# Attention with two window patterns and a gated unit: larger gated blocks, smaller convolution parts, and a new instruction order

## The chip, the cores and the metric

The kernel runs on one core of a Trainium2 chip. A core has TensorE (PE, matrix products), VectorE (DVE), ScalarE (ACT), GpSimd (POOL) and SyncE (SP, which here only issues DMAs), each with its own instruction queue, and 16 DMA engines. The metric is the device time of one execution in microseconds, the median of several runs; lower is better.

## The reference

Eight batches, eight heads, 576 positions, 64 numbers a head. Heads 0 to 3 attend to the last 32 positions, heads 4 to 7 to every fourth of the last 128. The result, 512 numbers a position, goes into a gated unit: a causal convolution over five positions, a channel at a time, through a sigmoid, times a product with `w_val`, and the whole through `w_out`.

```python
rel = pos[:, None] - pos[None, :]
mask_plain = (rel >= 0) & (rel < window)                       # window = 32
mask_dil = (rel >= 0) & (rel < window * dilation) & (rel % dilation == 0)   # dilation = 4
...
attn = np.exp(scores)
attn = attn / (np.sum(attn, axis=-1, keepdims=True) + 1e-09)
return np.matmul(attn, v).astype(np.float32)
...
x = np.ascontiguousarray(attn_out.transpose(0, 2, 1, 3)).reshape(B, S, H * D)
...
for k in range(K):                                             # K = 5
    gate_pre += conv_w[k][None, None, :] * xp[:, k:k + S, :]
gate = 1.0 / (1.0 + np.exp(-gate_pre))
val = x @ w_val
return (gate * val @ w_out).astype(np.float32)
```

## The kernel before

The kernel is written as a list of tasks. A task (`Task`) has a name, the engines that can do it with a planned duration on each, the tasks it depends on, and the buffers it uses (`Ten`, one of a small class of equal buffers whose sizes stand in `TUNE['n']`). `Plan` gives each task an engine, a place and its buffers. It can search an order itself (`run`); here it follows one that is written out, `ORDER`: 825 words, each a task's number and the letter of its engine (`p` PE, `a` ACT, `d` DVE, `g` POOL, `s` SP). The order in `ORDER` is the order of each engine's instructions; between engines, semaphores make a task wait for what it needs. `place` keeps a clock for each engine from the planned durations. These serve to choose a buffer (the one that comes free first), and to decide in `fill` where the constant products go: while the planned PE clock is below `TUNE['warm']` and a gap is planned, PE multiplies the zero tile `warm` (512 columns) into a PSUM buffer that is free.

PSUM is held as three double banks (`ps2`, called `pd` in the profile) and two single ones (`ps1`, `pu`).

For each batch two attention halves run, `plain` (heads 0 to 3) and `dilated` (heads 4 to 7). Both load q and k (`load_qk`, L832), turn them on PE (L977 plain, L1071 dilated), copy them to SBUF (`copy`, L908 ACT, L910 DVE, L912 POOL), make scores in parts of 64 rows by 128 columns of the array (L1001, L1113), take the exponential on ACT (`softmax_half`, L931), and multiply by the mask. A dilated mask is a product on DVE (L942); a plain one is either that or two selections on POOL (L814, L816 in `band`). Then follow the products with V (L1014; L1127 and L1136), the division on DVE (L1024, L1025; L1148, L1149), and a transpose back (L1034; L1158, L1161) into `xT`, which holds the attention's result with channels on partitions.

V reaches the plain half in two ways. For batches 0 and 1 (`FAST = 2`) it is loaded in rows of four positions (L846, L849) and spread to positions by products with a shifted identity (`plain_v`, L871 and L877), in two tasks of 16 products. For the others a slower load (L839) puts it there at once, and POOL clears the part ahead of the sequence (L964). V of the dilated half is loaded (L893, L899) and cast on POOL (L912).

`gated` works on half a batch, 288 positions, and two of the four groups of 128 channels at a time, so 32 times. The convolution (L1189) is 20 products with diagonal 64x64 parts, four in the array at once, of 288 columns; `conv_diag` holds the diagonals. ACT takes a tanh (L1199). The value products (L1207) are eight of 288 columns, and DVE joins both into `ya` (L1217). `outputs` takes 128 positions at a time: four products of 512 columns (L1234), an eviction on ACT (L1242) or DVE (L1244), a store (L1248).

`weights` loads `w_val`, `w_out` and the convolution's weights (L1259, L1299, L1301) and casts them; rows and columns of the weights are put in an order that fits the halves in which the convolution leaves the channels.

Of the kernel before, what the change touches and what calls it, by code (L numbers as in the profile page):

```python
# [9 lines left out]
BF16 = mybir.dt.bfloat16  # L10
# [227 lines left out]
 'warm': 45.0,  # L238
 'stall': 0.601,
 'ahead': 7.06,  # L240
# [49 lines left out]
 'n': {'vf': 4,  # L290
       'ps2': 3,
       'ps1': 2,
       'qk': 5,
       'vp': 2,
       'va': 4,
       'vb': 3,
       'vab': 2,
       'vbb': 2,
       'qTp': 2,
       'kTp': 1,  # L300
       'qTd': 3,
       'kTd': 3,
       'et': 13,
       'xn': 5,
       'gate': 7,
       'osb': 15,
# [6 lines left out]
30s 2g 11d 8d 29s 9d 67s 118s 16a 0g 4a 3g 6d 1d 7d 5g 66s 40p 42p 10d 15g 41a 43a 14g 119s 12g  # L313
36p 38p 39d 37a 17a 55p 48p 68s 44p 49a 56a 59p 45a 69s 74p 31s 60a 46d 75d 76a 77p 32s 127p 79a
125p 126d 78a 95p 91p 33s 128d 131p 96a 57d 84p 156s 129p 85a 80p 130d 92a 155s 70p 50d 132a 93g
157s 86d 81a 13d 61d 137p 133p 34g 82d 72p 134a 97d 71a 35g 47p 158s 73d 51p 138a 121s 18p 52d
144p 122s 62p 145a 120s 58p 148p 63d 163p 149a 208s 53p 19a 164d 87p 165a 20g 83p 98p 64p 88d 166p
65a 23s 21s 94p 54a 161p 150d 207s 99d 168a 124g 167a 180p 135d 162d 184p 181a 173p 89p 123g 245s
174a 159p 139d 185a 146d 186d 244s 151p 160a 90d 147p 100p 152d 136p 140p 24g 101a 169p 218p 141d
170a 220p 106p 219a 171d 22g 102p 107a 175d 114p 103a 221d 153p 293s 292s 176p 115a 182d 172p 216p  # L320
108p 177d 217a 154a 214p 27s 109d 187p 183p 215a 116p 188d 226p 142p 25s 227a 117d 178p 246s 233p
222p 143d 234a 248p 223a 179d 251p 250d 249a 189p 104p 252d 253a 265p 105d 110p 266a 190d 258p
111a 254p 267d 299p 329s 303p 259a 199p 304d 255a 28g 260g 195p 235d 200a 191p 228d 196a 193p 256g
26d 300d 112p 192a 194d 330s 305p 113d 197p 306a 301p 198d 717p 247g 209s 211s 269p 718a 237p 210s
257p 261p 238a 732p 262d 270a 331s 203p 733a 271g 224d 336p 204a 302d 333p 239d 337a 322p 335d
723p 323a 338d 212g 415s 334a 272p 268p 729p 724a 273d 213g 225p 263p 730a 229p 343p 230d 339p
726p 340a 264d 344a 240p 414s 727d 307p 354p 308a 231p 236p 274p 355a 241d 205p 332g 378s 275a
294s 341g 201p 206d 232a 345d 276p 295s 356g 202d 296s 346p 277a 342p 242p 347d 738p 377s 243a
350p 311p 309d 318p 351a 720p 739d 319a 416s 352d 421p 312a 324d 418p 423a 422d 388p 420a 353p
297g 357p 278p 358d 419a 499s 298g 721a 288p 279d 428p 289a 359p 389d 280p 429a 360d 435p 281a  # L330
424p 430g 384p 390p 436a 385d 290p 313d 391a 437g 348p 425a 463s 291d 310p 314p 386p 315d 282p
387a 349d 379s 417g 439p 407p 320d 381s 440a 735p 500s 283d 408a 321p 316p 441d 736a 325p 462s
392p 317a 326d 396p 747p 393a 409d 380s 442p 397a 327p 748d 464s 438p 361p 328a 394d 362a 741p
465s 443d 403p 284p 404a 426d 365p 466s 742d 285a 369p 398d 366a 431p 370a 427p 473p 432d 503p
551s 506p 548s 504a 383g 505d 373p 507a 722s 382g 501s 471p 374a 286p 472d 508a 405d 469p 287d
474a 395p 399p 520p 400d 513p 750p 514a 470d 521a 410p 751d 524p 547s 509p 525a 401p 406p 433p
402a 411d 371p 526g 510a 475p 372d 375p 476a 467g 434a 481p 636s 376d 477p 482a 632s 412p 558p
413d 367p 478a 559a 483d 502g 585s 560p 368d 488p 584s 561a 468g 492p 753p 522d 493a 515g 479d
444p 586s 754a 523p 527p 445d 363p 489a 511g 528d 556p 480p 484p 557a 364d 446p 490d 450p 447a
485d 744p 451a 494d 491p 756p 745a 554p 495p 555a 454p 496d 458p 455a 757d 562p 497p 563a 516p  # L340
758s 486p 498d 634s 512p 459a 588p 725s 517d 591p 589a 759p 593a 487d 550s 587g 456p 592d 752s
746s 518p 457d 633s 460p 519a 670s 637g 760d 549s 743s 590a 762p 755s 461d 553g 573p 763d 598p
594p 595a 780p 599a 596g 669s 529p 452p 781a 574a 448p 600g 453d 749s 530a 564d 768p 449d 765p
769a 770s 609p 766d 566p 605p 764s 567a 771p 740s 782s 606a 641p 767s 772d 535p 610a 607g 635s
539p 536a 611d 531p 642d 540a 552g 575d 543p 532a 568d 577p 643p 578a 671s 537p 544a 579d 761s
608p 644a 612p 538d 533p 613d 645p 601p 597p 646a 777p 602d 778a 565p 639p 569p 534d 640a 673p
570d 676p 674a 783p 675a 677d 678a 576p 571p 784d 580p 731s 572a 662p 734s 581d 679p 728s 614p
680a 774p 719s 663a 785s 681d 672g 658p 615d 683p 638g 541p 684a 659a 685d 582p 545p 542d 583a
775a 660d 647p 690p 546d 648a 603p 786p 691a 604d 661p 787d 788s 692g 694p 651p 695a 792p 664d
652a 696d 665p 620p 666d 616p 621a 649d 628p 617a 653d 624p 793d 795p 625a 794s 629a 686p 682p  # L350
# [52 lines left out]
class Plan:  # L403
# [71 lines left out]
    def fill(self, until):  # L475
# [3 lines left out]
        if not self.first.end or self.first.end + 0.1 > c:  # L479
            return  # L480
# [889 lines left out]
```

## Time and profile before

| | |
|---|---|
| median of three runs | 167.94 us (167.31 to 168.11) |
| the profiled execution: its own time | 168.98 us |
| the profiled execution: span from first to last instruction | 167.3 us |
| loads and stores | 42.99 MB moved, mean 257 GB/s |
| first 14 us: PE busy, DMA share | 8.71 us, 0.87 |
| from 138 us to the end: PE busy, DMA share | 25.38 us, 0.40 |

The profile is of one execution. Its page gives each engine's busy time as a share of the span, and the chain of work that ended last, followed back from the last instruction. A group of instructions is listed with its busy time, the mean duration of one, and the idle time before it. Products on PE overlap, so a group's busy time is less than its number times its mean, and the mean is longer than the distance from one start to the next. In a line on a stretch the first two numbers are its ends, the third its length, and then PE, PEld (weight loads), DVE, ACT and POOL follow with busy time and count; the last three are TensorE's granted clock, the share of the DMA engines' time and GB/s. In the chain in order of time a line has its start, its length and what it was; in a list of waits, who waited for whom: us in all, times, and the longest.

### The profile page before, as it was taken

To read this page: it belongs to the slowest core of one execution; us is meant where nothing else is said; L and a number is where in the kernel's file an instruction comes from. 1 tells how busy PE (TensorE), PEld (TensorE's weight loads), DVE (VectorE), ACT (ScalarE), POOL (GpSimd) and SP (SyncE) were. 2 spreads that over 40 slices of the span, in tenths; PEclk is the share of its full clock that TensorE was granted. 3 is DMA by queue.
4 is the path that set the end of the run, shared out by engine and by line. 5 is a ranking of instruction groups with operands and counts; after the bars stand their busy time and mean duration, and the time that the engine had idled before them with its cause. 6 is when DMAs were issued, how large, how long until landed. Compare 5 with 4: busy or idle time off the path is not lost.

```text
span 167.3 us, 6119 instructions
## 1 busy us (share of the span) xinstructions
PE 152.9 (91%) x2602; PEld 112.2 (67%) x2621; DVE 117.7 (70%) x250; ACT 110.1 (66%) x184; POOL 51.4 (31%) x86
## 2 busy tenths in 40 slices
PE   0898889989999999999997999999999999999991
PEld 0556677878776676786674876866687667785740
DVE  6127699989797888868757697784789787870520
ACT  4669567876847767777765885656686886357142
POOL 7802554430373370370030770009240221000000
PEclk9999999999999999999999999999999999999999
DMA  5999949999999999989999998179999902100995
GB/s 174 394 386 249 331 139 330 303 396 353 214 293 292 216 387 275 220 314 326 291 266 206 307 341 131 64 243 362 371 402 261 352 20 84 46 0 30 348 352 215
DMA packets 39442, 42.99 MB, mean 257 GB/s; under 512 B 20339, under 2 KB 27640, under 8 KB 39416
## 3 DMA queue, kind: packets, MB, share of 16 engines
q1 hardware_dynamic: 39376, 42.61, 84.7%
q8 instruction: 20, 0.33, 0.9%
q14 instruction: 6, 0.05, 0.1%
q10 hardware_dynamic: 40, 0.01, 0.0%
HBM read 33.17 MB, written 9.44 MB: 255 GB/s over the span
## 4 chain that ended last, share of the span: by engine, by line
PE 71%; DMA 15%; DVE 4%; SPq 4%; issue 2%; ACT 1%; POOL 0%; DVEq 0%; POOLq 0%
PE pd L1207 19%; PE pu L1234 18%; PE pd L1189 12%; DMA qk<-in_q_dram 8%; DMA vb<-in_v_dram 4%; PE pu L1071 3%; PE pd L1113 3%; PE pd L1014 3%; PE pd L1001 2%; PE pd L977 2%; DMA qk<-in_k_dram 2%; PE pu L1034 2%; PE pd L1127 2%; PE pu L1161 2%; SPq L899 2%
## 5 line engine op out<-in xcount | busy, mean ns | idle before, releaser
L931 ACT ACTIVATE et<-pd 128x576 bf16<-128x576 f32 x64 | 39.1, 652 | 13.8 <-PE pd L1113 6.5
L1207 PE MATMUL pd<-xT,w_val 128*128 128x288 bf16 x256 | 35.8, 286 | 0.3 <-DVE qTp L910 0.3
L1234 PE MATMUL pu<-w_out,ya 128*128 128x512 bf16 x126 | 34.1, 380 | 1.5 <-issue 0.8
L1217 DVE SCALAR_TENSOR_TENSOR ya<-gate,pd 128x576 bf16<-128x576 bf16 x32 | 23.7, 749 | 8.0 <-PE pd L1207 5.7
L1207 PEld LDWEIGHTS <-w_val 128*128 128x128 bf16 x256 | 23.7, 98 | 6.5 <-issue 0.6
L1199 ACT ACTIVATE gate<-pd 128x576 bf16<-128x576 f32 x32 | 20.3, 650 | 8.8 <-PE pd L1189 7.3
L1189 PE MATMUL pd<-xT,conv_diag 64*64 64x288 bf16 x640 | 23.0, 285 | 0.4 <-issue 0.2
L942 DVE TENSOR_TENSOR et<-et,mask_d 128x576 bf16<-128x576 bf16 x32 | 18.4, 586 | 3.1 <-ACT et L931 3.1
L814 POOL TENSOR_SCALAR_AFFINE_SELECT et<-et 128x576 bf16<-128x576 bf16 x15 | 11.6, 775 | 28.8 <-ACT et L931 25.6
L1234 PEld LDWEIGHTS <-ya 128*128 128x128 bf16 x144 | 12.2, 97 | 12.1 <-issue 0.9
L1189 PEld LDWEIGHTS <-conv_diag 64*64 64x64 bf16 x640 | 17.6, 106 | 3.4 <-issue 1.4
L1242 ACT ACTIVATE osb<-pu 128x512 f32<-128x512 f32 x21 | 12.6, 600 | 10.6 <-PE pu L1234 10.5
L1071 PE MATMUL pu<-perm_q,qk 128*128 128x128 bf16 x144 | 13.4, 231 | 5.2 <-DMA qk<-in_k_dram 4.7
L1025 DVE TENSOR_TENSOR xn<-pd,rec 96x768 bf16<-96x768 f32 x16 | 15.3, 954 | 0.7 <-DVE rec L1024 0.2
L908 ACT COPY xT<-pu 128x576 bf16<-128x576 bf16 x19 | 11.9, 644 | 5.7 <-PE pu L1161 2.8
L1071 PEld LDWEIGHTS <-qk 128*128 128x128 bf16 x144 | 9.9, 104 | 7.7 <-DMA qk<-in_k_dram 4.7
L1244 DVE TENSOR_SCALAR osb<-pu 128x512 f32<-128x512 f32 x15 | 10.3, 687 | 6.3 <-PE pu L1234 5.7
L1149 DVE TENSOR_TENSOR xn<-pd,rec 128x640 bf16<-128x640 f32 x16 | 13.2, 824 | 0.5
L912 POOL CAST vab<-va 128x1024 bf16<-128x1024 f32 x8 | 8.8, 1106 | 15.3 <-DMA va<-in_v_dram 15.3
L908 ACT COPY kTd<-pu 128x512 bf16<-128x512 bf16 (+1 forms) x12 | 9.0, 747 | 5.1 <-PE pu L1071 3.9
L816 POOL TENSOR_SCALAR_AFFINE_SELECT et<-et 128x576 bf16<-128x576 bf16 x15 | 11.5, 767 | 1.0
L942 DVE TENSOR_TENSOR et<-et,mask_p 128x576 bf16<-128x576 bf16 x17 | 10.0, 598 | 1.3 <-ACT et L931 1.2
(83 smaller groups left out, 209.1 us busy)
## 6 DMA issues: line engine op xcount, KB each, us to landing
qk<-in_k_dram SPq DMA_DIRECT2D x16, 576.0 KB, 6.8
qk<-in_q_dram SPq DMA_DIRECT2D x16, 576.0 KB, 6.7
out_dram<-osb SPq DMA_DIRECT2D x36, 256.0 KB, 3.5
va<-in_v_dram SPq DMA_DIRECT2D x10, 512.0 KB, 6.8
vp<-in_v_dram SPq DMA_DIRECT2D x6, 768.0 KB, 9.6
vb<-in_v_dram SPq DMA_DIRECT2D x16, 128.0 KB, 6.1
va<-in_moe_w_out_dram SPq DMA_DIRECT2D x6, 128.0 KB, 6.0
va<-in_moe_w_val_dram SPq DMA_DIRECT2D x2, 256.0 KB, 6.3
```

The lines of the kernel that those rows point to most:

```text
L908: nc.scalar.copy(out=out_, in_=in_)
L931: nc.scalar.activation(out=view(), in_=ps2[ps.idx][:, :, 0:HW], func=AF.Exp, scale=scale)
L942: nc.vector.tensor_tensor(out=ev, in0=ev, in1=m, op=ALU.mult)
L1025: nc.vector.tensor_tensor(out=xn[xt.idx][0:96].rearrange("p (h j) l d -> p h (j l) d", h=2), in0=a[:, :, :, 0:D], in1=rr[:, :, :, None].to ...
L1071: nc.tensor.transpose(out=ov[:, e], in_=a[:, i * 128:(i + 1) * 128], identity=perm_q[o])
L1149: nc.vector.tensor_tensor(out=xn[xt.idx][:, 0:5].rearrange("p n x d -> p x n d"), in0=a[:, :, :, 0:D], in1=rr[:, :, :, None].to_broadcast( ...
L1189: nc.tensor.matmul(out=ps2[pc.idx][64 * ob:64 * ob + 64, n, 0:HW], lhsT=conv_diag[rb, 2 * cp + n, kk, :], rhs=xT[xt.idx][rb, 2 * cp + n, s ...
L1199: nc.scalar.activation(out=gate[g.idx], in_=ps2[pc.idx][:, :, 0:HW], func=AF.Tanh, scale=0.5)
L1207: nc.tensor.matmul(out=ps2[pv.idx][:, n, 0:HW], lhsT=w_val[:, mc, c * 128:(c + 1) * 128], rhs=xT[xt.idx][:, mc, c0:c0 + HW], start=(mc == ...
L1217: nc.vector.scalar_tensor_tensor(out=ya[yt.idx][:, 2 * cp:2 * cp + 2, t0:t0 + HW], in0=gate[g.idx], scalar=1.0, in1=ps2[pv.idx][:, :, 0:HW ...
L1234: nc.tensor.matmul(out=ps1[po.idx], lhsT=ya[yt.idx][:, c, t0:t0 + 128], rhs=w_out[:, c, :], start=(c == 0), stop=(c == NCH - 1))
L1242: nc.scalar.activation(out=osb[ob.idx], in_=ps1[po.idx], func=AF.Copy, scale=0.5)
```

## The change

The gated unit works on blocks of 384 positions that go across the two batches of a pair, three for each pair: `BLOCKS`. So there are 24 pairs of convolution and value products instead of 32, of 384 columns instead of 288. The middle block reads two batches at once (`x_cols`), for which the `xT` buffers become one tile. In the two blocks of `FINE`, the second and third of the last pair, the convolution is one task of 80 products in parts of 32x32, 16 at once. For these the diagonals, identities, `w_val`'s columns and `w_out`'s rows of the last two groups of channels are put in a new order of 32; `w_val`'s casts are twelve copies instead of eight and `w_out` comes in twelve loads instead of seven.

The V spread of batches 0 and 1 is one task of 32 products: for the first and last blocks of 96 positions a product takes 64 rows only, and two run side by side.

Scores (`keys`) are made in parts of 64x64 wherever they stand next to a 64x64 convolution in PE's order (`share`): 13 plain and 4 dilated tasks of the 64.

The last output tile is made, evicted and stored in two halves of 256 columns.

`fill` places constant products by a measure of how active PE has been (`moved_by`, `TUNE['act']`), with new planned lengths, and only while the planned clock is below 34 instead of 45 us; two are asked for ahead of a first value product before that time. In the program there are ten (before, nine): six between the two q/k transposes of the first plain half and four behind them.

Buffer numbers change (`TUNE['n']`), and `ORDER` is a new list, of 792 words. In it 26 plain masks are on POOL (before, 15), DVE has 59 copies (41) and ACT 55 (65). `w_out`'s loads stand behind fewer q and k loads than before. PE has 2592 products (2621), and its array changes shape 131 times between products (134).

```diff
- 'warm': 45.0,
+ 'warm': 34.0,
+ 'act': 1.9,
+ 'guard': 2,
...
- 'n': {'vf': 4,
+ 'n': {'vf': 2,
...
-       'qk': 5,
+       'qk': 4,
...
-       'va': 4,
-       'vb': 3,
-       'vab': 2,
-       'vbb': 2,
+       'va': 3,
+       'vb': 4,
+       'vab': 4,
+       'vbb': 3,
...
     def fill(self, until):
...
+        c = max(self.clock[PE], self.first.end + 0.1)
+        u = 0.43 if c < 4.0 else 0.22
+        n = max(0, int((until - c - 0.05) / u))
+        heat = self.moved_by(None, end=until) + 0.213 * n
+        if heat < TUNE["act"]:
+            n += min(4, math.ceil((TUNE["act"] - heat) / 0.213))
...
+    def share(self, tasks):
+
+        run = []
+        for t in tasks + [None]:
+            if t and (t.form or t.mode == "64"):
+                run.append(t)
+                continue
+            if any(not u.form for u in run):
+                for u in run:
+                    if u.form:
+                        u.mode = u.leaves = "64"
+                        u.count *= 2
+            run = []
...
+    G = 32
+    MIX = [0, 2, 1, 3]
+    BLOCKS = [[(0, 384), (384, 768), (768, 1152)]] * 4
+    FINE = [(3, 1), (3, 2)]
...
+            for j in range(2):
+                for c in range(R):
+                    rows(j, slice(0, 64), c, c == R - 1)
+                    rows(j + 3, slice(64, 128), c, c == R - 1)
+            for j in (2, 5):
+                for c in range(R):
+                    rows(j, slice(0, 128), c, c == R - 1 and j == 2)
...
+    def keys(form):
+
+        parts = [slice(0, 128)] if form == "r64" else [slice(0, 64), slice(64, 128)]
+        return [(k, l) for k in parts for l in range(2)]
...
+        def conv_fine(eng):
+            for kk in range(K):
+                for n in range(NCH):
+                    for r in range(4):
+                        rb, ob = (slice(G * i, G * i + G) for i in (r, r ^ MIX[n]))
+                        d0 = G * ((r ^ MIX[n]) % 2)
+                        nc.tensor.matmul(
+                            out=ps2[pcs[n // 2].idx][ob, n % 2, 0:n_], lhsT=conv_diag[rb, n, kk, d0:d0 + G],
+                            rhs=x_cols(rb, n, kk - (K - 1)), start=(kk == 0), stop=(kk == K - 1))
...
+        for i, n0, n1 in [(i, 0, Dm) for i in range(last)] + [(last, 0, Dm // 2), (last + 1, Dm // 2, Dm)]:
...
+                    if turned:
+                        res += [nc.sync.dma_start(out=o[G * i:G * i + G],
+                                                  in_=w[heads[i // 2] * D + G - i % 2 * G:heads[i // 2] * D + 2 * G - i % 2 * G, :])
+                                for i in range(4)]
```

## The prediction

> **What bounds the kernel now.** I read the page's busy times and chain first, then the chain in order of time, then the groups by line and shape, the stages, and last the waits.
>
> ```profile
> span 167.3 us, 6119 instructions
> PE 152.9 (91%) x2602; PEld 112.2 (67%) x2621; DVE 117.7 (70%) x250; ACT 110.1 (66%) x184; POOL 51.4 (31%) x86
> ...
> PE 71%; DMA 15%; DVE 4%; SPq 4%; issue 2%; ACT 1%; POOL 0%; DVEq 0%; POOLq 0%
> ```
> ```profile
> 28.43 6.64 DMA qk<-in_q_dram
> 35.11 0.40 PE pu L1071 x4
> ...
> 94.32 0.98 PE pd L1207 x8
> ...
> 116.84 1.73 PE pu L1234 x8
> ...
> 120.28 2.58 PE pd L1189 x80
> ...
> 163.78 0.60 ACT osb L1242
> ```
> ```profile
> L1189 PEld LDWEIGHTS <-conv_diag 64*64 64x64 bf16 x640 | 17.6, 106 | 3.4 <-issue 1.4 <-DVE ya L1217 0.2
> L871 PE MATMUL pd<-va,spread 128*128 128x256 bf16 x32 | 4.0, 274 | 0.6 <-DMA va<-in_v_dram 0.4
> L1136 PEld LDWEIGHTS <-et 64*32 64x32 bf16 x128 | 2.0, 91 | 1.3 <-issue 0.4
> ```
> ```profile
> 14.00:43.00 29.00, 26.67 (x516) 21.46 (x517) 24.83 (x48) 20.66 (x35) 10.96 (x15) 1.00 0.95 301
> 43.00:138.00 95.00, 92.09 (x1639) 67.28 (x1647) 74.31 (x131) 67.89 (x115) 33.26 (x47) 1.00 0.96 268
> ```
>
> TensorE bounds it, from 35 us to the end; before that the chain runs through the loads (DMA 15%, SP's queue 4%). In the stage lines PE is the first number: 26.67 of 29 us and 92.09 of 95. The DMA share (0.95, 0.96) is as full, but the chain crosses it only up to 35.11.
>
> A busy PE is no price, so I take prices from the distance between starts. The chain gives eight products of 288 columns in 0.98 us, 122.5 ns each, and eight of 512 in 1.73, 216 each; hence 0.417 ns a column and 2.3 ns a product, and 384 columns cost 162.5. The 64x64 convolution runs four products at once: 80 are 20 rounds of 122.5 = 2.45 us, and one change of array shape makes the 2.58. Reading all starts, a product behind one of another array shape comes 92 to 97 ns late, nearly without exception; the program has 134 such changes, 12.7 us. The starts leave 6.7 us of real waiting after these: 4.2 before 43 us (0.6 of it at 35.11) and 1.33 in one place at 91.5. Products left out of the trace, 18 of the 144 at L1234, look like gaps and aren't counted.
>
> **The change, part by part**, as differences on the end.
>
> *Convolution.* Now 32 tasks x 5 rounds x 122.5 = 19.60 us. After: 20 tasks x 5 x 162.5 = 16.25, and two fine ones (blocks 1 and 2 of the last pair, 16 parts of 32x32 at once, 80 products each). No 32x32 part is in the trace. Below: 5 x 162.5 plus 16 starts at the 3.3 ns by which the four parts of L1189 follow each other, 0.87 us. Above: the densest 32 weight loads and products of the trace take 306 ns, 9.6 each; 160 of them are 1.54. I take 1.0, near the lower, since instructions that stand ready at L1189 start 1.7 ns apart. 16.25 + 2.0 - 19.60 = **-1.35** (-0.3 to -1.6).
>
> *Value products.* 256 x 122.5 = 31.36 becomes 192 x 162.5 = 31.20: **-0.16**. The output products keep their columns.
>
> *V spread of batches 0 and 1.* The 48 products of 256 columns cost 113 ns (16 in 1.97 us: 1.97 less one duration 0.274, over 15). Sixteen become pairs of 64-row parts that run at once, 2 x 8 pairs in place of 32 products: -16 x 113 = -1.81. But one task now waits for the small loads too, and it lies where loads set the chain. Bounds 0 and -1.8; I take **-1.7**, nearer the full one, as PE idles only 2.33 of 29 us there.
>
> *Scores in 64x64 parts beside a convolution* (17 of 64 tasks): the columns per round are the same, the instructions twice as many. At best 0; at 9.6 ns each, 13 x (24 x 9.6 - 122) + 4 x (32 x 9.6 - 172) = 1.4 + 0.5. I take **+0.4**, nearer the bottom for the 1.7 ns above. The form is there to spare shape changes; the two orders counted have 134 and 131: **-0.28**.
>
> *Tail.* The last output tile comes in halves. Evictions on ACT cost 652 ns for 576 columns and 600 for 512, so 392 for 256: -0.21. The span ends 2.88 us after the last eviction, with 256 KB to store; half of it I put at -0.24. **-0.45** (-0.2 to -0.6).
>
> *Constant products.* Nine become ten; none now lies ahead of the first q/k transposes of the plain heads, six lie between the two and four behind. The rule of two ahead of the first V finds no place before 34 us and adds none. Before, the first fillers start 427 ns apart at 5.65 us, and 216 apart at 11.13: PE ran at half speed until about 9.65, where the trace's granted clock begins at full. With less work early, ten at half speed instead of full cost 10 x 211 = 2.1 us; if the clock comes as before, nothing, as they stand in waiting time. I take **+0.3** (0 to +2.1). The Trainium skill (TensorE: Matmul & The Clock Gate, Part 1) says that PE stays at half rate until one free-running window of about 3.4 us was busy, and falls back after an idle one. An estimate by that page: one window missed here is the 2.1, and my sum would be 1.8 less.
>
> *Costed at nothing.* The w_val casts go from eight to twelve copies (459 ns each on POOL; half of them now on another engine): hidden, since V has other PE work ahead of it; else +0.9. The identity copies (234 ns, two more) hide behind POOL's 2.7 us wait for conv_w. w_out comes in twelve loads, not seven, and ahead of four q/k loads that it stood behind: five more issues at 0.60 to 0.77 us (four took 3.06) hold SP's queue 3.0 to 3.8 us, and those loads behind it. Gated work of batches 0 and 1 covers; uncovered, it is the fourth rival below. Eleven plain masks go from DVE (598 ns) to POOL (775 + 767), 15 to 26 of them; POOL is 31% busy. Eighteen copies move to DVE and ten leave ACT, both at about 70%. Nothing there is on the chain. PSUM pairs are held longer by a block of 384 but 24 times, not 32, for each of both products.
>
> *The new order* has waits of its own. At best the 2.5 us behind 35 us go; a bound above is in the rivals. I carry the 6.7 us over: **0**.
>
> Sum: -1.35 - 0.16 - 1.7 + 0.4 - 0.28 - 0.45 + 0.3 = **-3.24 us**. The span of 167.3 becomes 164.0; with the 1.7 us around it the profiled execution of 168.98 would be 165.7. The runs' median, 167.94, is 1.04 below that execution; the same difference gives **164.7**.
>
> **The rivals.**
>
> *Masks behind late V loads (slower).* POOL works in order, and its casts of V wait for landings:
>
> ```profile
> POOL vab L912 <- DMA va<-in_v_dram: 15.3, 5, 8.2
> POOL vp L964 <- DMA vp<-in_v_dram: 15.0, 3, 8.1
> POOL vbb L912 <- DMA vb<-in_v_dram: 11.3, 5, 9.1
> ```
>
> 41.6 us in 13 waits, 3.2 each. In the new order 13 places have a mask right behind such a cast, clear or weight cast, against about nine, and the products with V wait for the mask on a PE whose order is fixed. Against it: no PE wait before named a mask on POOL. A landing late past its cover stops PE for at most the mean 3.2 us; I take 2.5, as some PE work always lies between. Beyond 1.3 of them the gain is gone, and two give 164.7 + 5 = 169.7.
>
> *Weight loads of column parts run one after another.* L1189's 640 loads cover 17.6 us, 27.5 ns each, and L1136's 2.0, 15.6 each. In a row, a fine convolution is 80 x 15.6 = 1.25 us (+0.5 for both over my 1.0), and the scores are 13 x (12 x 27.5 - 122) + 4 x (16 x 27.5 - 172) = +3.8 where I took 0.4. The time is 164.7 + 0.5 + 3.4 = 168.6. Against it: at L1189 four loads start within 10 ns and each lasts 106, so they overlap. The Trainium skill (TensorEngine Tiling (Array Packing), Gotcha 2: Feature Incompatibilities) says that column tiling rules out the fast weight load, which speaks against all these small parts; by that rule alone this rival holds, and the trace, with whole rounds at 122.5 ns, doesn't show its cost.
>
> *Waits removed.* The new order keeps the savings and loses the 1.33 at 91.5, 0.6 at 35.1 and the small ones: 164.7 - 2.5 = 162.2.
>
> *The front is the loads'.* The V spread pays nothing (+1.7) and the five issues come through by a third (+1.1): 167.5, no change. For it: the chain to 35 us. Against it: PE is 92% busy from 14 to 43.
>
> **How the numbers follow.** The forecast, 164.7, has 0.57; its own range is 162.5 to 167.0 by the bounds of its terms. Waits removed 0.13, the front 0.10, serial weight loads 0.05, late masks 0.15. About 0.5% (0.84 us) can be told from no change: faster is below 167.1, slower above 168.8. Faster: 0.57 + 0.13 = 0.70. Same: 0.10 and half of the serial loads, which fall on the bound, 0.12 after rounding. Slower: the rest, 0.18. The range 161.3 to 168.8 leaves out most of the late masks, about 0.13, and few of the fastest.
>
> **What would show it.** Right: the fine convolution about 1.0 us in the chain, the value products 162.5 ns apart, scores of 64x64 near 0.13 to 0.17 us, PE idle before 43 us no longer than now, the last eviction near 0.39 us, no PE wait on a POOL mask. Wrong: starts 427 ns apart after 10 us, a fine convolution above 1.4 us, PE waits of over 1 us ended by POOL or a load, or a PE that stands still at new places between 43 and 138 us.

## The result: 3.9% slower, and the profile after

The changed kernel takes 174.16 us (median of four runs, 172.78 to 174.88), the kernel before, in runs on the same chip, 167.62 (166.70 to 168.11). The ratio is 1.0387, with a 95% interval of 1.0306 to 1.0468. The profiled execution took 174.03 us, with a span of 172.3; before it was 168.98 and 167.3. The time lies outside the forecast range, on the other side of no change. Some executions of a kernel take over 1.5% longer than its fastest, most of them at a lower granted clock, and the times and ratios below leave these out.

The head of the page of the changed kernel, its row of granted clock (40 slices of 4.3 us each, in tenths), and its chain by engine:

```profile
span 172.3 us, 6086 instructions
...
PE 153.4 (89%) x2571; PEld 103.8 (60%) x2592; DVE 118.9 (69%) x251; ACT 103.2 (60%) x167; POOL 64.6 (37%) x106
...
PEclk9999999659999999999999999999999999999999
...
PE 76%; DVE 8%; ACT 7%; issue 3%; POOL 3%; DMA 2%; ACTq 0%; DVEq 0%
```

PE idles 18.9 us of the span, where it idled 14.4 before. The chain now runs through VectorE and ScalarE (8% and 7%; before, 4% and 1%) and hardly through a load (2%; before, 15%). In the eighth and ninth slice, 30 to 39 us, TensorE ran at about half clock.

Two groups of the changed kernel, by line and shape (busy time, mean of one, and the idle time before them):

```profile
L1263 PE MATMUL pd<-xT,conv_diag 32*32 32x384 bf16 x160 | 2.4, 326 | 0.0
...
L920 PE MATMUL pd<-va,spread 64*128 64x256 bf16 x24 | 2.1, 272 | 0.0
```

The new products cost what was forecast. From start to start, a sixteen-part product follows the one before it by 11.2 ns, so a fine convolution takes 0.9 us (forecast 1.0); a value product of 384 columns takes 162.5 ns; a changed array shape still 92 to 97 ns.

Two stretches of the changed kernel (columns as in the section on the profile before):

```profile
14.00:43.00 29.00, 26.04 (x436) 18.37 (x437) 21.60 (x39) 17.36 (x28) 18.84 (x29) 0.88 0.92 252
43.00:138.00 95.00, 89.40 (x1623) 61.80 (x1636) 72.43 (x125) 65.94 (x108) 38.81 (x57) 1.00 0.95 265
```

From 14 to 43 us PE is busy nearly as long as before (26.04 us against 26.67), but at a granted clock of 0.88, and with 436 recorded products in place of 516. From 43 to 138 it is busy 2.7 us less. The waits, longest sums picked out:

```profile
POOL vab L967 <- DMA va<-in_v_dram: 8.1, 3, 4.3
...
POOL vp L1024 <- DMA vp<-in_v_dram: 1.3, 1, 1.3
PE pd L1061 <- ACT qTp L963: 1.3, 2, 1.1
PE pd L1075 <- ACT qTp L963: 1.3, 1, 1.3
PE pu L1095 <- DVE xn L1086: 1.2, 1, 1.2
...
PE pd L1297 <- ACT xT L963: 1.1, 1, 1.1
...
PE pu L1095 <- DVE vf L965: 1.0, 1, 1.0
```

POOL waits far less for loads of V than before (8.1 for `vab`, which was 15.3, and 1.3 for `vp`, which was 15.0), and no PE wait names a POOL mask. PE waits for copies, and in two places for a division or a cast on VectorE (`xn`, `vf`).

To place the loss, count the matrix work in each program: every product at 0.417 ns a column plus 2.4, divided by the number of parts that fit into the array beside it, constants left out. Then read from the starts when so much of it is left, counted from the end.

| | work, us | 100 us left, at | 20 us left, at | last product, at |
|---|---|---|---|---|
| before | 130.1 | 50.2 | 143.1 | 163.4 |
| after | 126.5 | 52.2 | 147.0 | 168.5 |

The change took away 3.6 us of work. Yet the first 26.5 us of work (the front) take 52.2 us, where 30.1 took 50.2: two us later, although 3.6 less was done. That makes 5.6 us lost in the front. The middle, 80 us of work in both, takes 94.8 us, not 92.9, and the last 20 us of work 21.5, not 20.3: 1.9 and 1.2 us lost. (Since the count is from the end, the same amount left isn't quite the same place in the two programs.)

### The profile page after: what moved, and what is told of

Same layout as the page of the kernel before. It is cut to its first block, busy times and chain, and to the rows that moved or that the text cites. A ratio compares the mean times of both kernels' runs of the same rounds, so it can differ in the third digit from the quotient of the medians.

```text
span 172.3 us, 6086 instructions
## 1 busy us (share of the span) xinstructions
PE 153.4 (89%) x2571; PEld 103.8 (60%) x2592; DVE 118.9 (69%) x251; ACT 103.2 (60%) x167; POOL 64.6 (37%) x106
## 4 chain that ended last, share of the span: by engine, by line
PE 76%; DVE 8%; ACT 7%; issue 3%; POOL 3%; DMA 2%; ACTq 0%; DVEq 0%
PE pd L1297 18%; PE pu L1325 16%; PE pd L1278 10%; PE pu L1132 6%; PE pd L1037 4%; PE pd L1174 3%; PE pd L1061 3%; PE pd L1075 3%; PE pd L1189 3%; DVE et L1002 3%; PE pu L1095 2%; DMA qk<-in_k_dram 2%; ACT et L991 2%; DVE qTp L965 2%; PE pd L1198 2%
## 5 line engine op out<-in xcount | busy, mean ns | idle before, releaser
L865 POOL TENSOR_SCALAR_AFFINE_SELECT et<-et 128x576 bf16<-128x576 bf16 x26 | 18.5, 712 | 65.1 <-ACT et L991 65.1
L1297 PE MATMUL pd<-xT,w_val 128*128 128x384 bf16 x192 | 34.3, 325 | 1.5 <-ACT xT L963 1.1
L1325 PE MATMUL pu<-w_out,ya 128*128 128x512 bf16 (+1 forms) x128 | 33.9, 373 | 1.9 <-issue 1.0
L1306 DVE SCALAR_TENSOR_TENSOR ya<-gate,pd 128x768 bf16<-128x768 bf16 x24 | 22.8, 950 | 12.3 <-PE pd L1297 9.3
L1289 ACT ACTIVATE gate<-pd 128x768 bf16<-128x768 f32 x24 | 19.0, 812 | 5.9 <-PE pd L1278 3.7
L1333 ACT ACTIVATE osb<-pu 128x512 f32<-128x512 f32 (+1 forms) x22 | 12.9, 593 | 15.2 <-PE pu L1325 15.1
L1278 PE MATMUL pd<-xT,conv_diag 64*64 64x384 bf16 x400 | 19.6, 334 | 0.2 <-ACT et L991 0.2
L867 POOL TENSOR_SCALAR_AFFINE_SELECT et<-et 128x576 bf16<-128x576 bf16 x26 | 19.0, 729 | 1.8
L1132 PE MATMUL pu<-perm_q,qk 128*128 128x128 bf16 x144 | 14.4, 242 | 5.1 <-DMA qk<-in_k_dram 4.7
L1086 DVE TENSOR_TENSOR xn<-pd,rec 96x768 bf16<-96x768 f32 x16 | 15.3, 954 | 0.6
L1335 DVE TENSOR_SCALAR osb<-pu 128x512 f32<-128x512 f32 (+1 forms) x15 | 9.8, 666 | 4.3 <-PE pu L1325 4.2
L965 DVE COPY xT<-pu 128x576 bf16<-128x576 bf16 x17 | 9.1, 542 | 3.7 <-PE pu L1095 2.1
L1174 PE MATMUL pd<-qTd,kTd 64*128 64x126 bf16 (+3 forms) x288 | 9.6, 202 | 1.3 <-ACT qTd L963 0.7
```

The lines of the kernel that those rows point to most:

```text
L865: nc.gpsimd.affine_select(out=dst, in_=dst, compare_op=ALU.is_ge, fill=0.0, base=base, pattern=pattern, channel_multiplier=-1)
L867: nc.gpsimd.affine_select(out=dst, in_=dst, compare_op=ALU.is_ge, fill=0.0, base=W - 1 - base, pattern=[[-a, n] for a, n in pattern], chan ...
L1086: nc.vector.tensor_tensor(out=xn[xt.idx][0:96].rearrange("p (h j) l d -> p h (j l) d", h=2), in0=a[:, :, :, 0:D], in1=rr[:, :, :, None].to ...
L1132: nc.tensor.transpose(out=ov[:, e], in_=a[:, i * 128:(i + 1) * 128], identity=perm_q[o])
L1174: nc.tensor.matmul(out=ps2[ps.idx][kb, l, c0:c0 + ln], lhsT=kTd[kt.idx][rb, k0 + kb.start:k0 + kb.stop], rhs=qTd[qt.idx][rb, cb, :, h, pr] ...
L1278: nc.tensor.matmul(out=ps2[pc.idx][64 * ob:64 * ob + 64, n, 0:n_], lhsT=conv_diag[64 * hb:64 * hb + 64, 2 * cp + n, kk, :], rhs=x_cols(sli ...
```

## The experiments

All times are medians of two to nine runs (two for e5, e12 and e18); a ratio is to the kernel before on the same chip, with its 95% interval. Kernels ran on different chips, so two of them are best compared by their ratios.

| | kernel | us | ratio |
|---|---|---|---|
| e1 | after, `conv_diag` in four instructions | 173.43 | 1.0374 (1.0321 to 1.0426) |
| e2 | after, both copies of a plain q or k on one engine | 172.35 | 1.0295 (1.0243 to 1.0348) |
| e3 | after, clock held by early constants | 173.62 | 1.0374 (1.0309 to 1.0439) |
| e4 | e1, e2 and e3 together | 170.40 | 1.0187 (1.0142 to 1.0233) |
| e5 | e2, four q/k loads ahead of `w_out` | 178.34 | 1.0638 (1.0553 to 1.0723) |
| e6 | old order, V spread and scores of the change | 171.58 | 1.0223 (1.0143 to 1.0303) |
| e7 | before, pairs on one engine | 168.40 | 1.0050 (1.0010 to 1.0089) |
| e8 | e6 with pairs on one engine | 173.49 | 1.0357 (1.0273 to 1.0441) |
| e9 | e2, four `xT` buffers | 169.26 | 1.0147 (1.0042 to 1.0251) |
| e10 | e2, convolution in 64x64 throughout | 170.68 | 1.0229 (1.0110 to 1.0349) |
| e11 | e4, e9 and e10 together | 169.96 | 1.0179 (1.0086 to 1.0272) |
| e12 | e2, e9 and e10 together | 168.90 | 1.0109 (1.0021 to 1.0197) |
| e13 | e9's smaller buffers, three `xT` | 172.18 | 1.0306 (1.0238 to 1.0373) |
| e14 | e12, few constants | 170.84 | 1.0212 (1.0137 to 1.0287) |
| e15 | e6, V spread earlier | 171.23 | 1.0271 (1.0190 to 1.0352) |
| e16 | e2, a `w_val` cast on ScalarE | 171.60 | 1.0243 (1.0174 to 1.0313) |
| e17 | e16, four `xT` buffers | 170.75 | 1.0161 (1.0093 to 1.0230) |
| e18 | e17, convolution in 64x64 throughout | 170.10 | 1.0133 (1.0041 to 1.0224) |

No version beats the kernel before. In the diffs below, words of the order are given by task name and engine.

**e1, e2, e3, e4: three suspects of the changed kernel, alone and together.** The trace of the changed kernel shows a VectorE mask beside POOL's `conv_diag`:

```profile
26.00 2.95 DVE L1002 TENSOR_TENSOR et<-et,mask_d 128x576 bf16<-128x576 bf16 x2
```
```profile
26.24 2.40 POOL L1376 TENSOR_TENSOR conv_diag<-ident,conv_w 128x1280 bf16<-128x1280 bf16 x1 [2.02 <-DVE conv_w L965]
```

Two masks take 2.95 us. The first starts before POOL's instruction and takes 0.45; the second takes 2.58. So e1 splits POOL's instruction:

```diff
-            e.tensor_tensor(
-                out=conv_diag.rearrange("p (u n) k d -> p u (n k) d", u=2),
+            for c in range(NCH):
+                e.tensor_tensor(
+                    out=conv_diag[:, c],
...
```

> The changed kernel with conv_diag made by four instructions on POOL instead of one. Theory A (a mask on DVE was held for 2.58 us while POOL made conv_diag, PE then waited 1.2 and 1.0 us at 30 and 32 us, and this quiet stretch sent the PE clock to half from 31.6 to 38.4 us): the mask is held for under 1 us, the two waits shrink to under 0.5 us each, the second stretch at half clock is gone, and the time falls by 4 to 6 us, to 168.5 to 170. Rival (the clock falls for want of PE work in that stage whatever DVE does): waits shrink by about 2 us, the clock still falls, 172 to 173.

173.43 us. The mask was freed (0.98 us), the waits of 1.2 and 1.0 us behind it went, and the clock stayed up from 25.1 us on, but the time didn't follow: new waits of 0.6 to 0.8 us for q/k loads, casts on POOL (V, `w_out`) and `xn` stand between 32 and 47 us.

The second suspect are the pairs. The two copies of a turned plain q or k read one PSUM tile, and in the trace the second is released by the first when they are on two engines; 10 of 16 pairs were so before, 14 are after. The chain of the changed kernel at 111 us:

```profile
110.72 0.64 PE pd L1037 x18
...
111.38 0.65 ACT kTp L963
...
112.05 0.76 DVE kTp L965
112.81 0.68 DVE qTp L965
...
113.51 0.65 ACT qTp L963
...
114.20 0.30 PE pd L1061 x6
```

Four copies run one after another, and PE waits 1.18 us. e2 gives each pair to one engine (14 copies change it; here one batch):

```diff
- Kp50/a Kp51/d Qp50/d Qp51/a
+ Kp50/a Kp51/a Qp50/d Qp51/d
```

> The changed kernel with both copies of a turned plain q or k on one engine (14 of 16 pairs are split over ACT and DVE there, and the second copy waits for the first). Theory B (four copies in a row, ACT, DVE, DVE, ACT, make PE wait 1.46 us at 71.7, 1.18 at 114.2, 0.67 at 85 and 0.61 at 125): those four waits go, the time falls by 3 to 4 us, to 170 to 171. Rival (the waits lie in the order and only move): less than 1 us.

172.35 us, 1.8 less than the changed kernel (1.5 by the ratios, whose intervals overlap; but every run of e2 lies below the fastest of the changed kernel). The same place in e2, and what is left of the wait (0.41 us by the starts):

```profile
109.66 1.15 PE pd L1062 x36
...
110.90 1.43 DVE qTp L990 x2
...
112.38 0.30 PE pd L1086 x6
```

The waits of 1.46, 0.28 and 0.39, 1.18 and 0.61 us at 71.7, 85, 114.2 and 125.4 us became 0.41 and 0.52 us at the last two, and the middle takes 92.3 us, not 94.8. So this is shown for the middle; the front is as late as it was (52.8 us with 100 us of work left).

e3 makes the zero tile first and adds constants ahead of late transposes:

```diff
+        if t.name in HOLD:
+            x = next(x for x in t.tens if x.cls in ("ps1", "ps2"))
+            self.constant(x.cls, x.idx, HOLD[t.name])
...
- mset#4/d ident/g ... first/d
+ first/d mset#4/d ident/g ...
```

> The changed kernel with the zero tile made first, so that constant products run from about 1.3 us on (nine ahead of the first load, nine more in the gaps up to 9 us), and with four constant products ahead of each of the two transposes that wait at 30 and 32 us. Theory C (the half clock itself costs the time): full clock from 5 to 9 us to the end, time falls by 3 to 5 us, to 169 to 171, with the two waits still there. Rival (PE waits for others in those stages and the clock costs nothing): the clock is full and the time within 1 us of 174.

173.62 us, with full clock from 6.3 us but for 16.5 to 20.0: the theory fell. The front ends at 52.1 us, with 100 us of work left, as in the changed kernel.

> conv_diag in four, pairs on one engine, and the early constant products together (without the four ahead of each late transpose). If A, B and C are separate and true: 164 to 167, no slower than the kernel before. If the loss lies elsewhere in the new order: above 169.

170.40 us, above the 169 that says the loss lies elsewhere. Against e2 it is 1.9 us less, and its front ends at 51.2 us instead of 52.8: what gained little alone gains together, which fits several things that bind the front at nearly the same time. That isn't shown: e4's is also the only trace of the four with the full clock from 5.5 us to the end.

**e5: loads of q and k ahead of `w_out`.** In the changed kernel SyncE's queue reads:

```profile
30.66 5.77 SPq L1391 DMA_DIRECT2D va<-in_moe_w_out_dram  x8
36.53 2.39 SPq L1397 DMA_DIRECT2D va<-in_moe_w_out_dram  x4
38.97 0.59 SPq L883 DMA_DIRECT2D qk<-in_q_dram  x1
```

and before:

```profile
36.65 0.33 SPq L1299 DMA_DIRECT2D va<-in_moe_w_out_dram  x1
37.03 4.33 SPq L1301 DMA_DIRECT2D va<-in_moe_w_out_dram  x6
```

Before, the four q/k loads landed at 36.6 to 42.6 us and `w_out` behind them by about 46; after, `w_out` had landed by 42.5 and the last of the four loads at 49.1.

```diff
- Lwo1/s Wo1/g Lwo0/s Wo0/g O0/p ... Lqp2/s ... Lkp2/s ... Lqd3/s ... Lkd3/s
+ Lqp2/s Lkp2/s Lqd3/s Lkd3/s Lwo1/s Wo1/g Lwo0/s Wo0/g O0/p ...
```

> The changed kernel with each pair of q or k copies on one engine, as in e2 (172.35 us), and with four loads moved: the q and k of the plain half of batch 2 and of the dilated half of batch 3 are issued ahead of w_out's twelve loads, and not behind them. Theory D (the front is the loads': in e2 SyncE is held by w_out's loads from 32.1 to 40.7 us, no q or k load is issued in that time, the DMA rate falls to 128 and 149 GB/s between 34 and 43 us, and PE then waits 0.88, 1.82, 0.30 and 0.90 us between 36.8 and 47.0): the wait on the DMA of qk near 47 us goes, the point at which 90 us of matrix work are left comes by 1 us or more earlier than in e2 (59.6 us), and the time is 170.8 to 171.6. Rival (the waits there are those of the w_val cast in VectorE's queue, and the output tiles O0 and O2 now come later): 172 to 173.5. Rival (the front is slack that the middle eats up again): no change, 172.1 to 172.6.

178.34 us. The test was badly made: the first output tile O0 stayed where it was in PE's order, ahead of the transposes, and PE waited 7.5 us at 53.1 for `w_out`. It says nothing on the theory, only that the order of the loads and the place of O0 are tied. The order of the loads stays untested.

**e6, e15, e7, e8: parts of the change in the old order.** e6 keeps the old order, blocks of 288, the old buffers and `fill`:

```diff
-    BLOCKS = [[(0, 384), (384, 768), (768, 1152)]] * 4
-    FINE = [(3, 1), (3, 2)]
+    BLOCKS = [[(0, 288), (288, 576), (576, 864), (864, 1152)]] * 4
+    FINE = []
...
- Pv00/p ... Pv01/p Ev00/a Ev01/d
+ Pv0/p Ev00/a Ev01/d
```

> The order of the kernel before, its buffers and its constants, with three of the changed parts: the V spread in one go on two halves of the array at once, 64x64 scores where they follow or precede a 64x64 product, and the last output tile in two halves. The gated unit stays in blocks of 288, the convolution in 64x64 parts throughout, w_val and w_out as before. Theory (the parts are worth what the forecast gave them, and the new order loses them): -1.7, +0.4 and -0.45 us against the kernel before, which is 165.3 to 166.6. Rival D (the front is set by loads, so that the V spread's 1.7 us do not count): 167.0 to 168.0. Rival (the spread in one go holds two buffers and comes later than its first part did): 168 to 169.5.

171.58 us, worse than each theory. The spread, now where its second part stood, no longer covers a `kTd` copy: PE waits 1.60 us at 16.5, and the clock halves from 16.6 to 20.1. A wait of another kind stands in the chain of e6:

```profile
88.16 0.81 PE pd L1294 x20
88.97 1.88 issue
90.85 0.38 PE pu L1148 x4
```

PE stands still for 1.88 us with nothing to wait for that the profile shows (last section). e15 moves the spread to where its first part stood:

```diff
- Lqp1/s Md001/d ... Mp000/d Pv0/p Mp011/a
+ Lqp1/s Pv0/p Md001/d ... Mp000/d Mp011/a
```

> e6 (171.6 us) with the V spread in one go at the place of the first of its two former parts, not the second. Theory (e6's loss is its wait of 1.60 us on the kTd copy at 16.5 us, which the first part used to cover, with the clock's fall behind it): that wait shrinks below 0.5 us, no half clock at 16.6 to 20.1, and the time is 166 to 169. Rival (the parts themselves cost more than they save in the old order): still 170.5 to 172.

171.23 us. The mechanism held, the time didn't follow: no half clock, the wait at 16.5 gone (0.88 at 15.6 for the exponential instead). The program has 1.7 us less work than before, and is 1.1 us ahead of the kernel before at a score product near 27 us, but 0.8 behind at the transpose for which PE used to wait on a load at 35.1. PE also stands still for 1.95 us at 88.9, where the kernel before has one such wait, of 0.39 us (last section). The V spread pays nothing in the old order either.

e7 and e8 put the pairs on one engine there (ten copies change; here one batch).

```diff
- Kp50/a Kp51/d
+ Kp50/d Kp51/d
```

> The kernel before with nothing of the change, only that the two copies of each turned plain q or k tile, which ten of its sixteen pairs have on two engines, are on one engine. Theory (two engines on one pair wait for each other, as e2 showed with 1.8 us for fourteen pairs): the waits at 42.4 and 68.4 us (0.31 and 0.42 us, on the qTp copy) go, and the time falls by 0.4 to 1.0 us to 166.6 to 167.2. Rival (e2's gain belongs to the new order, where those copies are late; in the old order they are early): no change, 167.3 to 167.8.

> e6 and e7 together: the order of the kernel before with the V spread in one go, the 64x64 scores, the halved last tile, and each pair of q or k copies on one engine. If both theories hold the gains add: 164.3 to 166.0, faster than either kernel. If the front is the loads' and the pairs do not matter in the old order: 167 to 168.

168.40 and 173.49 us: e7 is 0.5% slower than the kernel before, and e8's ratio lies above e6's, though the intervals overlap. What gained 1.8 us in the new order gains nothing in the old, so a rule of one engine for a pair is not general. The likely reason, that these copies had time to spare there, is not shown.

**e9 and e13: a wait on a buffer that isn't read.** The chain of the changed kernel at 100 us:

```profile
99.53 0.65 ACT et L991
100.18 0.54 ACT xT L963
...
100.76 0.81 PE pd L1297 x4
```

The value product of the block over batches 2 and 3 waits 1.26 us for a copy of batch 4. In the program its `xT` access goes from buffer 2 back to buffer 0 with a step of -5024 elements, and the trace releases it by the copy that writes from element 4064 on, in buffer 1. Nothing there is read: it looks as if the dependence is drawn over everything between the ends. With four buffers the two batches lie next to each other.

```diff
-       'xT': 3,
+       'xT': 4,
-       'vab': 4,
+       'vab': 3,
-       'osb': 17,
+       'osb': 16,
```

> e2 (172.35 us) with four xT buffers in place of three; the room comes from one buffer less of osb and of vab. Theory E (a wait on a buffer that is not read: the value product of the block that lies over batches 2 and 3 reads xT through one access pattern that goes from buffer 2 back to buffer 0, past buffer 1, and its instruction waits for the copy of batch 4's xT into buffer 1; with four buffers the two stand next to each other): the wait of 1.26 us at 99.7 us, which e2, e4 and the changed kernel all show on 'ACT xT', is gone, and the time is 170.9 to 171.4. Rival (the wait is taken over by the next late copy, of the exponentials that the same ScalarE queue holds): the wait stays at 0.8 us or more under another name and the time is 172 to 172.6.

> e2 (172.35 us) with one buffer less of vab and of osb, as in e9, but three xT buffers. If e9's gain is the fourth xT buffer's: 172 to 172.8, no change. If part of it came from the buffers taken away: 170 to 171.5.

169.26 and 172.18 us: the fourth buffer, not the smaller ones. The wait is gone in all kernels with four buffers, and stands at 1.25 to 1.27 us in all with three. But e9 gained 2.9 us on e13 (2.7 by the ratios), and its front ends at 50.9 us, not 52.5. Part of the rest is seen in VectorE's half of the `w_val` cast. In e2:

```profile
34.21 1.69 POOL L992 CAST w_val<-va 128x256 bf16<-128x256 f32 x6 [1.02 <-DMA va<-in_moe_w_val_dram]
35.85 0.71 POOL L890 TENSOR_SCALAR_AFFINE_SELECT et<-et 128x576 bf16<-128x576 bf16 x1
...
38.19 0.71 POOL L892 TENSOR_SCALAR_AFFINE_SELECT et<-et 128x576 bf16<-128x576 bf16 x1
```
```profile
35.95 3.03 DVE L990 CAST w_val<-va 128x256 bf16<-128x256 f32 x6 [1.96 <-DMA va<-in_moe_w_out_dram]
```

and in e9:

```profile
32.44 1.85 POOL L992 CAST w_val<-va 128x256 bf16<-128x256 f32 x6
```
```profile
33.56 1.22 DVE L990 CAST w_val<-va 128x256 bf16<-128x256 f32 x6 [0.26 <-DMA va<-in_moe_w_val_dram]
```

The cast waits for its own load. The last part of that load lands at 35.83 us in e2, at 35.65 in e13 and at 33.44 in e9, and VectorE starts 0.12 us later each time, in e9 in the midst of POOL's copies. (The view for e2 names a load of `w_out`, which counts on the same semaphores.) In e2 and e13 VectorE idles 1.96 and 2.37 us for it and then takes 3.03 and 3.08, beside four mask selections on POOL; in e9 it takes 1.22. The normalisation behind the cast held PE for 1.82 us in e2. Why the load lands 2.2 to 2.4 us earlier in e9 isn't shown; 0.7 us of it against e2 is that it was issued earlier.

**e10, e11, e12, e14.** e10 takes out the sixteen parts and their order of weights:

```diff
-    FINE = [(3, 1), (3, 2)]
+    FINE = []
...
-            t, lw = wload("wo", moe_w_out, pr, h0, h1, TUNE["wo"], pr == 1)
+            t, lw = wload("wo", moe_w_out, pr, h0, h1, TUNE["wo"], False)
...
- Cf71/p
+ C710/p C711/p
```

> e2 (172.35 us) with the sixteen-part convolution undone: the last two blocks in 64x64 parts like the others, w_val cast in four copies a pair and not six, w_out in seven loads and not twelve. By the prices of the products alone this costs 2 x (2 x 0.8 - 0.9) = 1.4 us: 173.7. Theory F (SyncE's twelve loads hold up the q and k loads of batches 2 and 3, and the casts hold up VectorE): SyncE's stretch on w_out shrinks from 8.5 us to about 5, the PE waits between 36 and 48 us (3.9 us in e2) shrink by 1 to 2.5 us, and the time is 171.2 to 172.6, that is, the sixteen parts earn nothing. If they also delay the gates, which start only when the whole sixteen-part product is done: 170.5 to 171.2.

170.68 us, 1.7 less than e2 (1.1 by the ratios, whose intervals overlap) in spite of 1.6 us more work. The PE waits from 36 to 48 us fell from 3.9 to 0.4; but here too the `w_val` load landed early, at 33.15 us, and the copies took 1.26, as in e9, so the gain can't be put down to the loads of `w_out` alone.

> e4 (170.4 us: conv_diag in four instructions, pairs on one engine, the constants early) with the repairs of e9 and e10. If their gains add: e4 less 1.3 us (E) and less 0 to 1.2 (F): 168.0 to 169.1. If what is left of the loss is in the front, which none of them touches but e10 through the loads, it ends no lower than 168.5. Below 167.5 it would beat the kernel before, and then the new order would be sound once these waits are out.

> The changed kernel with the three repairs that each gained alone: pairs on one engine (e2), four xT buffers (e9), 64x64 convolution throughout with w_out and w_val as before (e10). If the gains add: 172.35 - 3.1 - 1.7 = 167.6, the time of the kernel before within 0.5 us. If the xT repair gained only its wait of 1.3 us and e9's remainder was the front's jitter: 169.0 to 169.6. If another loss stands behind them: above 169.6.

> e12 with the constant products cut from twelve to four: none are added for the clock's sake, and those that fill a gap are counted at 0.43 us each (half rate, as the trace has them at 11.6 to 14.2 us) and not at 0.22. If the constants hold the clock up and are worth their time: slower than e12 by 0.5 to 2 us, with a stretch of half clock in the records before 40 us. If they only stand in the way of the transposes at 14.2 us, and the front waits for loads afterwards anyway: the same as e12 within 0.5 us. If the transposes' 1.9 us reach the end: faster by 1 to 2 us.

e11 took 169.96 us, e12 168.90, e14 170.84. In e11 nothing adds to e4 (1.0179 against 1.0187). e12 is the lowest of all by its ratio; if the gains added, it would take the time of the kernel before within 0.5 us, and its interval starts 0.35 us above that time, so whether they add stays open. e14 fills only gaps, at the half-rate length:

```diff
- 'act': 1.9,
+ 'act': 0.0,
...
-        u = 0.43 if c < 4.0 else 0.22
+        u = 0.43 if c < 14.0 else 0.22
```

Four constants instead of twelve gained nothing; the intervals overlap.

**e16, e17, e18: the cast off VectorE.**

```diff
- Ep111/a ... Lwv0/s Lwv1/s Wv1/d
+ Lwv0/s Lwv1/s Wv1/a Ep111/a ...
```

> e2 (172.35 us) with VectorE's half of the w_val cast on ScalarE, ahead of the fourth exponential there (ScalarE stands idle from 31.9 to 33.3 us in e2). Three xT buffers, sixteen-part convolution as in the change. Theory G (VectorE's cast collides with GpSimd's and holds up the normalisation and the mask behind it): the PE waits of 0.88 and 1.82 us on w_val and xn at 36.8 and 40.0 us go, TKp2 starts 1 us or more earlier than in e2 (47.0 us), and the time is 170.3 to 171.3. Rival (the twelve loads hold the front, and the wait moves to w_out or qk): TKp2 stays within 0.5 us and the time is 171.9 to 172.7.

> e16 with four xT buffers (one less of vab and of osb). If the collision is what e9 was lucky to miss, this is e9's time, 168.5 to 169.8, and e16 less 1.3 us. If the two add to more: 167.5 to 168.5. If e9's gain lay elsewhere: above 170.

> e17 with 64x64 convolution throughout and the weights loaded as before. Theory F (fewer loads, gates that start after half of the product, against 1.4 us of products): e17 less 0 to 1.2 us, 167.5 to 169.5. If e10's gain of 1.7 us was the collision missed, as its trace suggests (its w_val copies took 1.26 us): e17 plus 0.5 to 1.4 us, 169.5 to 171. Below 167 it would beat the kernel before.

e16 took 171.60 us, between the theory's time and the rival's. In the traces of e16 and e17 the waits on `w_val` and the `xn` behind it are gone, as the theory said; but e16's interval overlaps e2's, so no gain is shown. e17 is 0.8% faster than e16, 1.4 us by the ratios, which fits the `xT` wait at its own price of 1.26 us, though these intervals overlap too. e18 equals e17 within the intervals: the sixteen parts with all that they need earn nothing that these runs can tell. e9's further 1.6 us (2.9 less 1.26) have no single cause that was shown.

## Why the prediction was wrong, step by step

**The step that failed is "the new order: 0".** It carried the 6.7 us of waits over. The time rose by 6.5 us while the work fell by 3.6, so about 10 us came in as waits and as products at half clock. The traces hold 8.7 of it (the execution traced before was 1.4 us above the median): 5.6 in the front, 1.9 in the middle, 1.2 at the end. In the middle the cause is shown: 1.8 us by pairs on two engines (e2) and 1.26 by the `xT` tile (in all kernels of the new order with three buffers, in none with four). With both out, e9 goes from 100 to 20 us of work left in 91.0 us, 1.9 less than the kernel before; the work there is the same by the count, so this is less waiting, not the saving of the larger blocks. The sections ahead of the prediction name the one tile for `xT`; the prediction gave it no price. In the front the cause stays open.

**V spread, -1.7.** Bounds 0 and -1.8 were right, the choice wrong: PE's busy share from 14 to 43 us didn't show that PE was the limit. e15 has 1.7 us less work and doesn't end earlier.

**Costed at nothing: casts and loads.** In the changed kernel VectorE's `w_val` cast was hidden, as said: it took 1.03 us and waited for nothing, since its load had landed at 33.77 and VectorE came to it at 35.30. In e2 and e13, where the load landed late, it cost VectorE some 4 us (1.96 idle and 3.03 busy in e2). For the q/k loads the five more issues were the wrong price: all twelve loads of `w_out` now stand ahead, SyncE is on them from 30.66 to 38.92 us, and three of the four q/k loads, whose landing can be read in both traces, come 5 to 10 us later. In the changed kernel no PE wait of over 0.2 us names them. In e1, e2, e3, e9 and e17 PE waits 0.6 to 0.9 us for a q/k load near 46 us, and in e9 2.1 us for the cast of `w_out`. So the fourth rival, "the front is the loads'", may have the right place; its 2.8 us are half of what the front lost, and no run shows that loads cause it (e5 is void).

**Constant products, +0.3 (0 to +2.1).** Six of them run at 11.6 to 14.2 us, 427 ns apart, the half rate; the transpose behind them starts at 14.36, while its k had landed at 11.4. The clock came full at 14.5, not 9.65, and fell back from 31.6 to 38.4. That is the upper bound's mechanism, but neither holding the clock (e3) nor fewer constants (e14) gained alone. The Trainium skill (TensorE: Matmul & The Clock Gate, Part 1), cited in the prediction, has the rate go up after a busy window of about 3.4 us and down after an idle one. The traces agree with that length: half-rate stretches behind the start last 3.4 or 3.5 us each in e1, e3, e6 and e12, and one of 6.8 in the changed kernel.

**Convolution, value products, scores, shape changes.** Right in size: 3.6 us of work against 3.2 for convolution, value products and V spread; the count takes a sixteen-part convolution at 0.8 us and not 0.9 to 1.0, which is most of the difference. Of the 3.6, the V spread is 1.7 and the two fine convolutions 1.6; the larger blocks alone save 0.3. But the gates behind a sixteen-part convolution start only at its end, and with its loads and casts it is worth nothing that the runs can tell (e18 against e17).

**Tail, -0.45.** The half eviction takes 0.38 us, as forecast; but the span ends 3.1 us after the last eviction (before, 2.88), so half the bytes bring nothing there, and PE waits 0.36 us for a buffer. In all, the last 20 us of work take 1.2 us more.

**The rivals.** Late masks: no; PE never waited for a POOL mask, and POOL waited less for V. Serial weight loads: no; 11.2 ns from product to product, not 15.6. The Trainium skill (TensorEngine Tiling (Array Packing), Gotcha 2: Feature Incompatibilities) rules out the fast weight load here, and no cost of that is seen. Waits removed: the opposite. That the slower side had only 0.18 came from looking for one late mechanism, where the order itself was the change.

**What stays open** is the front, the largest part of the loss. It ends between 50.9 and 52.8 us in e1 to e4, e9, e13 and e17, whichever wait is taken away. The order of the loads was not tested, since e5 was void. The falling clock may cost time there or only show a front that idles: e2's four runs took 172.39 us at a mean granted clock of 0.967 and 171.70 to 172.52 at 1.0, which speaks for the second, but is one run.

## What to carry to other kernels

An instruction order is a part of the work, not a detail of it: price each wait that a new order can make, above all two engines on one tile, one access that steps over a buffer in use, and work of VectorE beside POOL's. In a stage with many waits, less matrix work may gain nothing (the V spread here), and taking out one wait shows the next; take several out together before you judge one. Count too where a saving lies: here nearly all of it was the V spread, in a front that waits, and two convolutions at the end, and the larger blocks themselves saved 0.3 us.

## What the runs showed of the hardware

**VectorE waits for POOL's whole instruction.** The mask that takes 0.45 us alone took 2.58 when it came 0.13 us behind the start of `conv_diag` on POOL, and ended 0.3 us after it. Beside POOL's mask selections in e2, four of VectorE's six `w_val` copies took 0.72 to 0.75 us, each ending about 0.1 us after a selection; the other two took 0.21 and 0.28. The selections themselves took 0.70 to 0.84 us. The Trainium skill (SBUF — State Buffer, SBUF: two separate sides) says that the two share a port pair as a lock that the first holder keeps for the whole instruction, where VectorE runs in a two-port mode or reads two inputs from SBUF. The traces agree for the mask and the copies.

**PE seems to starve for instructions.** The page lists 20 or 21 packets of 16 KB on a queue called "instruction", one for each 256 of PE's products and weight loads. Eight waits with no releaser, 0.38 to 1.95 us, all stand at the same place of such a block, to within a few instructions, and 2.5 to 2.8 us after a packet started: at 83.7 before, 90.9 in e6, 90.0 in e7, 49.0 and 91.1 in e8, 88.3 in e14, 88.9 in e15, 53.6 in e17. They are all the waits with no releaser of over 0.33 us between 20 and 165 us in all kernels. The cause is read from their place; no run changes the supply of instructions. The Trainium skill (Runtime: NRT & Kernel Launch, Instruction fetch mechanics) calls this fetch mostly hidden; in these eight places, if the reading is right, it isn't. The longest, over 1 us, are in e6, e8 and e15, the kernels in the old order whose 64x64 scores take twice the products.
